# Late one-hots and the tail's table kept in program place on VectorE, and a portion's lists loaded expert by expert, in a convolution and mixture-of-experts kernel

## The chip, the cores and the metric

The kernel runs on one core of a Trainium2 chip. Its time is the device time in microseconds (us), from a set of runs; a profiled execution beside them shows where it goes. TensorE multiplies, VectorE (DVE) and ScalarE (ACT) move results out of PSUM, GpSimd (POOL) issues the indirect transfers, and SyncE (SP) issues most of the others. Each of these engines works off its own stream of instructions in order.

## The reference, cut to what matters

```python
w = softmax(weight, axis=-1)                    # [8 heads, 7 taps]
out[b, s, h*24:(h+1)*24] = sum_k w[h, k] * x_pad[b, s + k, h*24:(h+1)*24]   # causal, 7 taps
x = out.reshape(23040, 192)
g = argmax(x @ w_group)                         # 4 groups
e = argmax(x @ w_expert[g])                     # 4 experts in each group: 16 in all
y[token] = p_group * p_expert * (relu(x[token] @ w1[g, e]) @ w2[g, e])      # 192 -> 1024 -> 192
```

Each of the 23,040 tokens goes through one of 16 experts, which is known only once its logits are there.

## The kernel before

**Units.** The tokens are cut into 18 units, 0 to 17, of 4, 8 or 12 blocks of 120 tokens; units 8 to 17 have 12 blocks each. A unit (`unit`) is a Python generator. It convolves its blocks on TensorE, turns them, makes the logits, and routes on VectorE (L501 to L530); ACT then stores the convolved tokens to DRAM (`xcd`, L532). After some empty steps it works out each token's place in its expert's list (L545 to L557) and makes one-hots of that place, in halves of six blocks: `ohl` (L567), `ohr` (L571) and `ohv` (L575). TensorE multiplies these into a list of token numbers (L589), VectorE writes it out (L596, L598), and POOL scatters it into the table `idtab` in DRAM (L601). Each `yield` ends a step; steps are taken in between the matmuls of the expert stage, at a rate (`rate`, from `stages`) that has units done in time.

**Portions and slots.** The expert stage works on slots of 256 tokens of one expert. Slots come in portions: portion 0 (one slot for each expert) needs units 0 to 4, portion 1 (two for each) units 0 to 11, and portion 2 (two for each) all 18. `open_portion` loads the lists of token numbers of a portion from `idtab` into the tile `idp` (L1017: one transfer for each of the 16 experts on SP, from an address in a register). What is left over after portion 2 goes through a tail of 18 slots, 9 of them smaller, which a table (`table`) on VectorE and DRAM describes: for each tail slot its expert's weights and its place in `idtab`. `open_tail` makes the table and loads the tail's lists (L1035), a step at a time.

**A slot.** `open_slot(i + 2)` is called during slot i. It loads the expert's weights (L622 to L626), and POOL gathers the tokens from `xcd` (L673). `turn` transposes them (L686, L687) into `xa` and `xb` (L688 to L693). Four times `hidden` (L704, into `ph`, three PSUM banks) and `back` (L722, L726, into `po`, two banks) follow; ACT and VectorE split each result of `hidden` in `hh` and `hl` (L709, L710). VectorE splits the weights too (L639, L647, L654). At the end `ys` is made from `po` by ACT (L784) and VectorE (L785), and POOL scatters it to the output (L775). The next slot's first `back` needs `po` free, thus both `ys` of the slot before.

**Order.** The program gives an order, but the tool that builds the kernel sets each engine's final order itself: it simulates the kernel, and an instruction whose inputs are there in that simulation may go ahead of earlier ones that have to wait. `tc.keep_in_program_order(ins)` ties an instruction behind the instruction that was written just before it for the same engine. Transfers issued by SP and ACT count on a small set of semaphores that are handed out in turn; who takes one waits until the transfer that had it before has landed.

Of the kernel before, what the change touches and what calls it, by code (L numbers as in the profile page):

```python
# [20 lines left out]
P = 128  # L21
BT = 120
# [14 lines left out]
def conv_moe_kernel(  # L37
# [16 lines left out]
    PINA = True  # L54
    PINB = True
    PINW = True

    def pin(on, ins):

# [75 lines left out]
    UG = [0, 5, 6, 1, 5, 8, 0, 5, 6, 0, 5, 7, 0, 5, 6, 2, 5, 10]  # L135
    SK = [8, 8, 6, 11, 10, 9, 9]
    KPRE = [2, 150, 155, 160, 162, 20]
    CEU = 0
    CEH = (1, 3, 5, 7)
    PF = 1  # L140
# [235 lines left out]
    def unit(u, pre=None):  # L376
# [110 lines left out]
        def bc(a, n):  # L487
            return a.unsqueeze(len(a.shape)).broadcast_to([*a.shape, n])
# [40 lines left out]
        nc.vector.scalar_tensor_tensor(out=se, in0=se, scalar=1e-9, in1=sg, op0=ALU.add, op1=ALU.mult)  # L529
        nc.vector.reciprocal(out=xc[0:Q, 0:nb, 0], in_=se)  # L530
        xcw = xcd[t0:t0 + nb * BT, :].rearrange("(b p) d -> p b d", p=BT)
        SE.dma_start(out=xcw, in_=xc[0:BT, 0:nb, 0:XW])  # L532
        for _ in range(rest):
            yield
        while any(need <= u and pi not in idps for need, pi in needs.items()):
# [24 lines left out]
        halves = []  # L560
        for b0 in range(0, nb, HB2):
            n = min(HB2, nb - b0)
            ohl = pa.tile([P, HB2, P], F16, name="ohl", bufs=2)
            ohr = rt.tile([P, HB2, LH], F16, name="ohr", bufs=1)
            ohv5 = pa.tile([P, HB2, LH], F16, name="ohv", bufs=2)
            bs = slice(b0, b0 + n)
            nc.vector.tensor_tensor(  # L567
                out=ohl[0:Q, 0:n], in0=iop[0:Q].unsqueeze(1).broadcast_to([Q, n, P]), in1=bc(posb[0:Q, 0, bs], P),
                op=ALU.is_equal,
            )  # L570
            nc.vector.tensor_tensor(  # L571
                out=ohr[0:Q, 0:n], in0=ior[0:Q].unsqueeze(1).broadcast_to([Q, n, LH]), in1=bc(posb[0:Q, 1, bs], LH),
                op=ALU.is_equal,
            )
            OHE.tensor_tensor(  # L575
                out=ohv5[0:Q, 0:n], in0=ohr[0:Q, 0:n], in1=bc(vals[0:Q, bs], LH), op=ALU.mult)
            halves.append((b0, n, ohl, ohv5))
        rows = rt.tile([P, E + 1], F32, name="rows")
        rowi = rt.tile([P, 1], I32, name="rowi")
# [226 lines left out]
    flags = const.tile([P, 2], F32, name="flags")  # L806
    flagi = const.tile([P, 2], I32, name="flagi")

    def table(first=None, nbig=NBIG, nsmall=NSMALL):


# [5 lines left out]
        c = {n: const.tile([P, 1], F32, name=f"tc{g}_{n}") for n in ("j", "m1", "m2", "oa", "ob", "k", "ja", "jb")}  # L817
        ti = const.tile([P, E], I32, name=f"tb{g}_i")
        ji = const.tile([P, 1], I32, name=f"tc{g}_i")
        v = nc.vector  # L820

        def ts(out, in_, s1, op0, s2=None, op1=None):
            if op1 is None:
                v.tensor_scalar(out=out, in0=in_, scalar1=s1, scalar2=None, op0=op0)
            else:
                v.tensor_scalar(out=out, in0=in_, scalar1=s1, scalar2=s2, op0=op0, op1=op1)

        def tt(out, a, b, op):
            v.tensor_tensor(out=out, in0=a, in1=b, op=op)

        def stt(out, a, s, b, op0, op1):
            v.scalar_tensor_tensor(out=out, in0=a, scalar=s, in1=b, op0=op0, op1=op1)
# [9 lines left out]
        nc.gpsimd.iota(ti, pattern=[[1, E]], base=0, channel_multiplier=0)  # L842
        v.tensor_copy(out=t["eid"], in_=ti)
        v.memset(t["one"], 1.0)
        base = cons if first is None else first
        tt(t["rem"], ends[:, nends[0]], base, ALU.subtract)
        if first is None:


            cnt = rt.tile([P, UB * NG, EG], F32, name="dd").rearrange("p m e -> p (m e)")  # L850
            most = const.tile([P, 1], F32, name="most")
            for h in range(2):
                us = slice(h * NU // 2, (h + 1) * NU // 2)
                cn = cnt[:, 0:NU // 2 * E].rearrange("p (u e) -> p u e", e=E)
                tt(cn, ends[:, us.start + 1:us.stop + 1], ends[:, us], ALU.subtract)
                v.tensor_reduce(out=most if h == 0 else flags[:, 0:1], in_=cnt[:, 0:NU // 2 * E], axis=AX.X, op=ALU.max)
            tt(most, most, flags[:, 0:1], ALU.max)
            ts(flags[:, 0:1], most, float(SLOT), ALU.is_gt)
            ts(flags[:, 1:2], most, float(SLOT), ALU.is_le)
            ts(t["rem"], t["rem"], flags[:, 1:2], ALU.mult)  # L860
        slots(t["nf"], P - 1 if first is None else SLOT - 1)
        slots(t["ns"], SLOT - 1)
        tt(t["ns"], t["ns"], t["nf"], ALU.subtract)
        for n, pe, st in (("nf", "pa", "sa"), ("ns", "pb", "sb")):
            v.tensor_tensor_scan(t[pe], t["one"], t[n], 0.0, ALU.mult, ALU.add)
            tt(t[st], t[pe], t[n], ALU.subtract)
# [2 lines left out]
        ts(c["oa"], t["pa"][:, E - 1:E], -float(nbig), ALU.add, 0.0, ALU.max)  # L869
        ts(c["ob"], t["pb"][:, E - 1:E], -float(nsmall), ALU.add, 0.0, ALU.max)  # L870

        ts(c["m1"], c["j"], float(nbig), ALU.is_ge)
        ts(c["m2"], c["j"], float(ntail), ALU.is_ge)
        tt(c["k"], c["m1"], c["m2"], ALU.subtract)
        stt(c["ja"], c["m2"], -float(nsmall), c["j"], ALU.mult, ALU.add)
        stt(c["ja"], c["k"], -1024.0, c["ja"], ALU.mult, ALU.add)
        stt(c["k"], c["j"], -float(ntail), c["oa"], ALU.add, ALU.is_lt)
        stt(c["k"], c["k"], 1024.0, c["oa"], ALU.mult, ALU.add)
        tt(c["k"], c["k"], c["m2"], ALU.mult)
        stt(c["jb"], c["j"], -float(nbig), c["k"], ALU.add, ALU.subtract)  # L880
        for st, pe, j, m in (("sa", "pa", "ja", "ma"), ("sb", "pb", "jb", "mb")):
            ts(t["r"], t[pe], c[j], ALU.is_le)
            stt(t[m], t[st], c[j], t["r"], ALU.is_le, ALU.subtract)
# [4 lines left out]
        tt(t["q"], t["ma"], t["mb"], ALU.add)  # L888
        tt(t["q"], t["q"], t["eid"], ALU.mult)
        v.tensor_reduce(out=c["k"], in_=t["q"], axis=AX.X, op=ALU.add)  # L890
        ts(ent[:, 0:1], c["k"], float(D), ALU.mult)
        ts(ent[:, 1:2], c["k"], float(F), ALU.mult)

        ts(c["ja"], c["ja"], float(SLOT), ALU.mult, -float(DUMMY), ALU.add)
        stt(t["q"], t["sa"], -float(SLOT), base, ALU.mult, ALU.add)
        stt(t["q"], t["q"], c["ja"], t["ma"], ALU.add, ALU.mult)
        stt(t["r"], t["nf"], float(SLOT), base, ALU.mult, ALU.add)
        stt(t["r"], t["r"], -float(DUMMY), t["mb"], ALU.add, ALU.mult)
        tt(t["q"], t["q"], t["r"], ALU.add)
        v.tensor_reduce(out=c["k"], in_=t["q"], axis=AX.X, op=ALU.add)  # L900
        ts(ent[:, 2:3], c["k"], float(DUMMY), ALU.add)
# [24 lines left out]

    def stages(u):
        q = units[u][1] // QB
        return 1 + 8 + (2 * FRH if u >= FRU else 0) + sum(gaps(u)) + 3 * q + 1 + (LISTLAG if u >= NEED else 0)

    SKEW1 = 8
    LIVE1 = 3
# [54 lines left out]
    def open_tail():  # L987
# [4 lines left out]
        for j in range(NTAIL):  # L992
# [4 lines left out]
            tail_ids(row, idps["tail"][:, j], 2 if j < NBIG else 1)  # L997
            yield

    def open_portion(pi):  # L1000
        need, spe = portions[pi]
        rows = spe * 2
        idp = const.tile([P, E, rows, 1], I32, name=f"idp{pi}")
        if pi == 0:
            pin(PINI, IQ.dma_start(
                out=idp,
                in_=idtab[0:E * CAP].rearrange("(e r) c -> e r c", e=E)[:, 0:P * rows, :].rearrange(
                    "e (p r) c -> p e r c", r=rows),
            ))
        else:  # L1010
            ci = const.tile([1, E], I32, name=f"ci{pi}")
            nc.vector.tensor_copy(out=ci, in_=cons[0:1])
            _, base = nc.values_load_multi_w_load_instructions(
                ci, engines=[ET.SP], min_val=0, max_val=DUMMY - P * rows, skip_runtime_bounds_check_because=OOB_WHY,
            )
            for e in range(E):
                nc.sync.dma_start(  # L1017
                    out=idp[:, e],
                    in_=idtab[bass.ds(base[e], P * rows), :].rearrange("(p r) c -> p r c", r=rows),
                )  # L1020
        idps[pi] = idp
        consume(spe * SLOT)
        if pi + 1 == len(portions):
            late.append(open_tail())
# [38 lines left out]
    def open_slot(i):  # L1063
# [16 lines left out]
        if pi == "tail":  # L1080
            W = tail_weights(i)
            ids = idps["tail"][:, e]
            known = N
        else:
            W = pre.pop(e if pi == 0 else None, None) or weights(e * D, e * F, PENG(pi, e)) if s == 0 else opened[i - 1][0]
            ids = idps[pi][:, e, 2 * s:2 * s + 2]
            known = sum(n for _, n in units[:portions[pi][0]]) * BT
        for q in range(i + 1, i + 1 + TAHEAD):
# [21 lines left out]
    open_slot(1)  # L1110
    for e in range(2, 2 + PRE2):
        pre[e] = weights(e * D, e * F)
    for k in range(AHEAD):
        step()
    while opened[0][0]["todo"]:
        split_one(opened[0][0])
    unit_banks[:] = [(pm, "pm")]
    lead[:] = SKEW2, LIVE2
    turned[0] = turn(gathered[0])
    pinned[0] = False  # L1120
    pend = []
    tick = 0
# [10 lines left out]
    for i, (pi, e, s) in enumerate(plan):  # L1133
# [7 lines left out]
        for f2 in range(steps):  # L1141
# [27 lines left out]
            for q in range(f2, NF // 2, steps):  # L1169
                k = (q + 2) % 4  # L1170
                if q < 2:
                    split_one(W, k)
                elif i + 1 < len(plan):
                    split_one(opened[i + 1][0], k)
            if i + 1 < len(plan):
                if f2 == n - 1:
                    turned[i + 1] = turn(gathered[i + 1], tiles(i + 1))
# [93 lines left out]
```

## Time and profile before

| | |
|---|---|
| runs | 1166.22 us median of 3 (1163.81 to 1169.93) |
| the profiled execution | 1157.9 us; span from first to last instruction 1156.1 us |
| TensorE busy, mean granted clock | 96% of the span, 0.991 of full speed |
| VectorE, ScalarE, GpSimd busy | 70%, 60%, 43% |

The busy share of TensorE is high, but it is not the same everywhere: the rows below go by stretches. A row of the timeline gives the start in us from the start of the span, the duration, the engine, the line, and in brackets the idle time of the engine before it and what ended that.

### The profile page before, as it was taken

The page shows a single profiled execution, that of the slowest core. Times are in us where ns is not written, and L with a number is a line of the kernel's source. Part 1 is how long each engine was busy: PE and PEld are TensorE (multiplying, and loading weights), DVE is VectorE, ACT ScalarE, POOL GpSimd, SP SyncE. Part 2 cuts the span into 40 slices and gives each one's busy share as a digit, 9 for nine tenths or more (in the row PEclk, how much of TensorE's full clock was granted, in tenths as well). Part 3 has the DMA queues.
Part 4 walks back from the last instruction along what each step waited for, and adds up shares of the span by engine and source line. Part 5 has one row for each costly group of instructions (what it writes and reads, how often), then busy time and mean ns, then how long its engine had stood idle before and what let it go on. Part 6 is the DMA issues. An engine that isn't in the chain of part 4 may idle for free.

```text
span 1156.1 us, 23806 instructions
## 1 busy us (share of the span) xinstructions
PE 1105.5 (96%) x8468; PEld 1076.4 (93%) x8468; DVE 804.7 (70%) x1668; ACT 689.2 (60%) x1374; POOL 494.2 (43%) x443
## 2 busy tenths in 40 slices
PE   6887999989999999999999999999999999999996
PEld 5777999989999999999998999999999999989986
DVE  4777788877867666666678565666666666688874
ACT  5474666657565555655554555656555555677873
POOL 2121232435344443333344444444444445577773
PEclk9899999999999999999999999999999999999998
DMA  8869699889775554536364564544444546399970
GB/s 191 227 180 280 156 233 233 221 183 263 218 186 149 150 171 115 139 114 169 96 155 108 155 199 132 142 133 139 133 141 132 141 120 169 107 249 267 257 198 19
DMA packets 167212, 195.63 MB, mean 169 GB/s; under 512 B 22500, under 2 KB 144333, under 8 KB 167086
## 3 DMA queue, kind: packets, MB, share of 16 engines
q1 hardware_dynamic: 125006, 140.41, 46.0%
q0 software_dynamic: 18752, 35.85, 10.9%
q10 hardware_dynamic: 23328, 17.80, 6.4%
q8 instruction: 67, 1.10, 0.4%
q14 instruction: 59, 0.48, 0.1%
HBM read 158.79 MB, written 36.58 MB: 169 GB/s over the span
## 4 chain that ended last, share of the span: by engine, by line
PE 76%; DVE 8%; DMA 6%; issue 4%; ACT 3%; POOL 1%; SPq 0%; another core or an unknown queue 0%; POOLq 0%; ACTq 0%; DVEq 0%
PE ph L704 31%; PE po L722 20%; PE po L726 9%; PE pm L426 3%; PE pm L466 2%; DMA xg<-xcd,idpt 2%; PE pm L686 1%; PE pm L687 1%; DVE hl L710 1%; PE pm L445 1%; PE ph L739 1%; DVE cw L654 1%; PE pm L469 1%; DMA rawc<-in_moe_w 1%; DVE ohl L567 1%
## 5 line engine op out<-in xcount | busy, mean ns | idle before, releaser
L722 PE MATMUL po<-cw,hh 128*128 128x384 f32 x1424 | 442.3, 368 | 6.4 <-DVE ys L785 6.3
L704 PE MATMUL ph<-xa,ah 128*128 128x256 f32 x1424 | 390.1, 296 | 6.6 <-DVE xa L689 3.4
L775 POOL DMA_INDIRECT out<-ys,idp x160 | 169.2, 1057 | 449.2 <-DVE ys L785 336.6
L710 DVE SCALAR_TENSOR_TENSOR hl<-ph,hh 128x512 fp32r<-128x512 f32 x356 | 240.9, 685 | 169.9 <-ACT hh L709 155.8
L726 PE MATMUL po<-cw,hl 128*128 128x192 f32 x1424 | 356.8, 251 | 0.0
L709 ACT ACTIVATE hh<-ph 128x512 fp32r<-128x512 f32 x356 | 210.7, 594 | 212.6 <-PE ph L704 157.3
L704 PEld LDWEIGHTS ph<-xa,ah 128*128 128x128 f32 x1424 | 270.9, 190 | 9.6 <-DVE xa L689 3.6
L722 PEld LDWEIGHTS po<-cw,hh 128*128 128x128 f32 x1424 | 268.5, 189 | 10.3 <-DVE ys L785 8.2
L726 PEld LDWEIGHTS po<-cw,hl 128*128 128x128 f32 x1424 | 272.5, 191 | 1.6
L673 POOL DMA_INDIRECT xg<-xcd,idp x160 | 186.0, 1163 | 57.1 <-issue 28.7
L704 PE MATMUL ph<-xb,bh 128*128 128x256 f32 x712 | 202.0, 284 | 1.0 <-DVE xb L693 1.0
L704 PE MATMUL ph<-xb,bl 128*128 128x256 f32 x712 | 202.0, 284 | 0.0
L704 PE MATMUL ph<-xa,al 128*128 128x256 f32 x712 | 201.2, 283 | 0.0
L704 PEld LDWEIGHTS ph<-xa,al 128*128 128x128 f32 x712 | 136.5, 192 | 2.2
L704 PEld LDWEIGHTS ph<-xb,bh 128*128 128x128 f32 x712 | 136.2, 191 | 1.2 <-DVE xb L693 1.2
L704 PEld LDWEIGHTS ph<-xb,bl 128*128 128x128 f32 x712 | 136.9, 192 | 0.0
L654 DVE TENSOR_TENSOR cw<-rawc,cw 128x768 fp32r<-128x768 f32 x114 | 105.2, 953 | 14.9 <-ACT cw L653 11.9
L639 DVE TENSOR_TENSOR al<-raw,ah 128x1024 fp32r<-128x1024 f32 x57 | 70.8, 1242 | 35.8 <-ACT ah L638 19.6
L653 ACT ACTIVATE cw<-rawc 128x768 fp32r<-128x768 f32 x114 | 91.2, 839 | 3.0 <-DMA rawc<-in_moe_w 3.0
L785 DVE SCALAR_TENSOR_TENSOR ys<-po,xg,ys 128x192 f32<-128x192 f32 x187 | 76.0, 415 | 24.4 <-ACT ys L784 16.5
L692 ACT ACTIVATE xb<-pm 64x256 fp32r<-64x256 f32 x98 | 36.0, 368 | 94.8 <-DVE xa L689 89.1
L784 ACT ACTIVATE ys<-po,xg 128x192 f32<-128x192 f32 x187 | 76.1, 418 | 22.7 <-PE po L726 12.0
(223 smaller groups left out, 1552.5 us busy)
## 6 DMA issues: line engine op xcount, KB each, us to landing
rawc<-in_moe_w SPq DMA_DIRECT2D x114, 384.0 KB
raw<-in_moe_w SPq DMA_DIRECT2D x57, 512.0 KB
raw<-in_moe_w SPq DMA_DIRECT2D x114, 256.0 KB
xcd<-xc ACTq DMA_DIRECT2D x13, 1085.6 KB
xin<-in_x SPq DMA_DIRECT2D x7, 1134.0 KB
xc<-in_moe_w SPq DMA_DIRECT2D x18, 384.0 KB
xin<-in_x SPq DMA_DIRECT2D x6, 1039.5 KB
xin<-in_moe_w SPq DMA_DIRECT2D x9, 512.0 KB
```

What stands on the lines that cost most here:

```text
L639: eng.get(k, nc.vector).tensor_tensor(out=al, in0=ra, in1=ah.bitcast(F32), op=ALU.subtract)
L653: pin(PINW, nc.scalar.activation(out=cw[:, fs, 0, :], in_=rc[k - 2], func=AF.Copy))
L654: eng.get(k, nc.vector).tensor_tensor(out=cw[:, fs, 1, :], in0=rc[k - 2], in1=cw[:, fs, 0, :].bitcast(F32), op=ALU.subtract,)
L673: nc.gpsimd.indirect_dma_start(out=xs[:, t, :], out_offset=None, in_=xcd[0:known, :], in_offset=bass.IndirectOffsetOnAxis(ap=ids[:, t, 0:1 ...
L704: nc.tensor.matmul(out=hp[:, j], lhsT=wgt[:, fs], rhs=xx, start=i == 0, stop=i == len(ops) - 1)
L709: nc.scalar.activation(out=hh, in_=hp, func=AF.Relu)
L710: nc.vector.scalar_tensor_tensor(out=hl, in0=hp, scalar=0.0, in1=hh.bitcast(F32), op0=ALU.max, op1=ALU.subtract,)
L722: nc.tensor.matmul(out=oo[t][:, 0:2 * D], lhsT=hh[:, j, ts], rhs=cw[:, f].rearrange("p a d -> p (a d)"), start=f == 0, stop=False,)
L726: nc.tensor.matmul(out=oo[t][:, 0:D], lhsT=hl[:, j, ts], rhs=cw[:, f, 0, :], start=False, stop=f == NF - 1,)
L775: nc.gpsimd.indirect_dma_start(out=outviews[nscat[0] % len(outviews) if view is None else view], out_offset=bass.IndirectOffsetOnAxis(ap=i ...
L784: nc.scalar.activation(out=ys[:, t, :], in_=oo[t][:, D:2 * D], func=AF.Copy, scale=g)
L785: nc.vector.scalar_tensor_tensor(out=ys[:, t, :], in0=oo[t][:, 0:D], scalar=g, in1=ys[:, t, :], op0=ALU.mult, op1=ALU.add,)
```

## The change

One-hots of units 8 and later (`LP = 8`) are held: each is tied behind the VectorE instruction written before it. Their second half is written three steps after the first (`HGAP = 3`). The instructions of the tail's table are held too, the table has 11 more `yield`s, and its steps are also taken once within each slot of portion 2. The list loads of portions 1 and 2 are no longer written all at once in `open_portion`: `open_slot` writes those up to the expert after the one that it opens. `stages` counts the three steps. `LG`, `TB` and `SEV` are given values (0, 0 and 99) with which their code does nothing.

```diff
+    def hold(on, ins):
+        return tc.keep_in_program_order(ins) if on else ins
...
+    SEV = 99
+    TB = 0
+    HGAP = 3
+    LP = 8
+    LG = 0
+    IDN = 2
...
         for b0 in range(0, nb, HB2):
             n = min(HB2, nb - b0)
+            if u >= LP and b0:
+                for _ in range(HGAP):
+                    yield
...
-            nc.vector.tensor_tensor(
+            hold(u >= LP, nc.vector.tensor_tensor(
                 out=ohl[0:Q, 0:n], in0=iop[0:Q].unsqueeze(1).broadcast_to([Q, n, P]), in1=bc(posb[0:Q, 0, bs], P),
                 op=ALU.is_equal,
-            )
+            ))
...
+    class InOrder:
+        def __init__(self, on):
+            self.on = on
+        def __getattr__(self, name):
+            return lambda *a, **k: hold(self.on, getattr(nc.vector, name)(*a, **k))
...
-        v = nc.vector
+        v = InOrder(first is None)
...
         slots(t["nf"], P - 1 if first is None else SLOT - 1)
+        yield
         slots(t["ns"], SLOT - 1)
         tt(t["ns"], t["ns"], t["nf"], ALU.subtract)
+        yield
...
-        return 1 + 8 + (2 * FRH if u >= FRU else 0) + sum(gaps(u)) + 3 * q + 1 + (LISTLAG if u >= NEED else 0)
+        return 1 + 8 + (2 * FRH if u >= FRU else 0) + sum(gaps(u)) + 3 * q + 1 + (LISTLAG if u >= NEED else 0) + (HGAP + 2 * LG if u >= LP else 0)
...
+    idget = {}
+    def lists(pi, n):
+        while idget.get(pi) and E - len(idget[pi]) < n:
+            idget[pi].pop(0)()
...
-            for e in range(E):
-                nc.sync.dma_start(
-                    out=idp[:, e],
-                    in_=idtab[bass.ds(base[e], P * rows), :].rearrange("(p r) c -> p r c", r=rows),
-                )
+            idget[pi] = [lambda e=e: nc.sync.dma_start(
+                out=idp[:, e],
+                in_=idtab[bass.ds(base[e], P * rows), :].rearrange("(p r) c -> p r c", r=rows),
+            ) for e in range(E)]
...
             W = pre.pop(e if pi == 0 else None, None) or weights(e * D, e * F, PENG(pi, e)) if s == 0 else opened[i - 1][0]
+            lists(pi, e + IDN)
             ids = idps[pi][:, e, 2 * s:2 * s + 2]
...
+            if f2 == 2 and late and pi == len(portions) - 1 and len(idps) == len(portions):
+                next(late[0], None)
```

`ohr` and `ohv` are held in the same way as `ohl`, and nine further `yield`s stand between the later groups of the table's instructions.

## Rows read from the trace of the kernel before

**Rows 1.** Stretches: length, busy us of TensorE, weight loads, VectorE, ScalarE, GpSimd; granted clock.
```profile
260.00:628.00 368.00, 361.62 (x2841) 354.78 (x2840) 262.54 (x557) 212.07 (x422) 151.11 (x133) 1.00 0.58 157
628.00:1005.00 377.00, 377.00 (x2933) 376.99 (x2932) 239.59 (x386) 213.19 (x389) 167.45 (x158) 1.00 0.50 140
```
**Rows 2.** Waits of TensorE from 100 to 1005 us: total, times, longest.
```profile
PE po L722 <- DVE ys L785: 6.3, 6, 1.6
PE ph L704 <- DVE hl L710: 3.2, 1, 3.2
```
**Rows 3.** Timeline of TensorE around 250 us.
```profile
253.95 0.39 PE L704 MATMUL ph<-xa,ah 128*128 128x256 f32 x1 [3.20 <-DVE hl L710]
...
254.97 0.41 PE L704 MATMUL ph<-xa,ah 128*128 128x256 f32 x1
```
**Rows 4.** Timeline of ScalarE around 250 us.
```profile
252.15 0.32 ACTq L532 DMA_DIRECT2D xcd<-xc  x1
252.57 1.08 ACT L709 ACTIVATE hh<-ph 128x512 fp32r<-128x512 f32 x2 [7.50 <-DMA idp<-idtab]
```
**Rows 5.** The stretch after that wait; the last three numbers begin with the clock.
```profile
254.00:260.00 6.00, 6.00 (x32) 5.71 (x33) 5.33 (x7) 4.54 (x9) 0.00 (x0) 0.72 0.75 160
```
**Rows 6.** The list loads: duration min/median/max in ns, first and last start.
```profile
L1017 SPq DMA_DIRECT2D idp<-idtab x32: 238/333/1973, 247.4 to 628.7; - x32
```
**Rows 7.** Waits of SP's queue over the span: total, times, longest.
```profile
SPq L623 <- DVE al L639: 119.6, 27, 13.5
SPq L1017 <- DMA idtab<-lsi,rowi: 10.3, 2, 5.9
```
**Rows 8.** Timeline of TensorE: its six waits for `ys` from 260 to 628 us.
```profile
297.49 0.45 PE L722 MATMUL po<-cw,hh 128*128 128x384 f32 x1 [0.56 <-DVE ys L785]
...
323.40 0.44 PE L722 MATMUL po<-cw,hh 128*128 128x384 f32 x1 [1.58 <-DVE ys L785]
...
358.60 0.44 PE L722 MATMUL po<-cw,hh 128*128 128x384 f32 x1 [1.41 <-DVE ys L785]
...
496.62 0.45 PE L722 MATMUL po<-cw,hh 128*128 128x384 f32 x1 [0.37 <-DVE ys L785]
...
611.58 0.44 PE L722 MATMUL po<-cw,hh 128*128 128x384 f32 x1 [1.25 <-DVE ys L785]
...
623.44 0.45 PE L722 MATMUL po<-cw,hh 128*128 128x384 f32 x1 [1.15 <-DVE ys L785]
```
**Rows 9.** Timeline of VectorE, unit 13's one-hots at 355 us.
```profile
355.86 0.95 DVE L567 TENSOR_TENSOR ohl<-iop,posb 120x768 f16<-120x768 f32 x1
...
357.86 0.35 DVE L575 TENSOR_TENSOR ohv<-ohr,vals 120x192 f16<-120x192 f16 x1
358.13 0.41 DVE L785 SCALAR_TENSOR_TENSOR ys<-po,xg,ys 128x192 f32<-128x192 f32 x1
```
**Rows 10.** Timeline of VectorE, the table from 615 us: its first and last here.
```profile
615.56 0.23 DVE L824 TENSOR_SCALAR pos<-pos 128x16 f32<-128x16 f32 x1
...
620.99 0.15 DVE L824 TENSOR_SCALAR tb_e<-tc_k 128x1 f32<-128x1 f32 x1
```
**Rows 11.** Timeline of an undisturbed slot's end, VectorE and then TensorE.
```profile
699.47 0.96 DVE L785 SCALAR_TENSOR_TENSOR ys<-po,xg,ys 128x192 f32<-128x192 f32 x2
...
701.77 0.34 PE L722 MATMUL po<-cw,hh 128*128 128x384 f32 x1
```
**Rows 12.** Waits of TensorE from 0 to 100 us: total, times, longest.
```profile
PE ph L589 <- DVE ohv L575: 2.9, 1, 2.9
```
**Rows 13.** Timelines: unit 12's last `ohv`, its list's matmuls, slot 16's gather and turn.
```profile
293.42 0.34 DVE L575 TENSOR_TENSOR ohv<-ohr,vals 120x192 f16<-120x192 f16 x1
...
308.65 0.47 PE L589 MATMUL pm<-ohv,ohl 120*128 120x32 f16 x12
...
302.61 1.47 POOL L673 DMA_INDIRECT xg<-xcd,idp  x1 [0.30 <-ACT ta L447]
...
318.09 0.38 ACT L688 ACTIVATE xa<-pm 128x256 fp32r<-128x256 f32 x1
```

More of the change, by code (lines that the diff above doesn't have):

```diff
@@ L531, in unit @@
         xcw = xcd[t0:t0 + nb * BT, :].rearrange("(b p) d -> p b d", p=BT)
-        SE.dma_start(out=xcw, in_=xc[0:BT, 0:nb, 0:XW])
+        (nc.sync if u >= SEV else SE).dma_start(out=xcw, in_=xc[0:BT, 0:nb, 0:XW])
         for _ in range(rest):
@@ L566, in unit @@
             bs = slice(b0, b0 + n)
-            nc.vector.tensor_tensor(
+            hold(u >= LP, nc.vector.tensor_tensor(
                 out=ohl[0:Q, 0:n], in0=iop[0:Q].unsqueeze(1).broadcast_to([Q, n, P]), in1=bc(posb[0:Q, 0, bs], P),
                 op=ALU.is_equal,
-            )
-            nc.vector.tensor_tensor(
+            ))
+            if u >= LP:
+                for _ in range(LG):
+                    yield
+            hold(u >= LP, nc.vector.tensor_tensor(
                 out=ohr[0:Q, 0:n], in0=ior[0:Q].unsqueeze(1).broadcast_to([Q, n, LH]), in1=bc(posb[0:Q, 1, bs], LH),
                 op=ALU.is_equal,
-            )
-            OHE.tensor_tensor(
-                out=ohv5[0:Q, 0:n], in0=ohr[0:Q, 0:n], in1=bc(vals[0:Q, bs], LH), op=ALU.mult)
+            ))
+            hold(u >= LP, OHE.tensor_tensor(
+                out=ohv5[0:Q, 0:n], in0=ohr[0:Q, 0:n], in1=bc(vals[0:Q, bs], LH), op=ALU.mult))
             halves.append((b0, n, ohl, ohv5))
@@ L857, in table @@
             tt(most, most, flags[:, 0:1], ALU.max)
+            yield
             ts(flags[:, 0:1], most, float(SLOT), ALU.is_gt)
@@ L861, in table @@
         slots(t["nf"], P - 1 if first is None else SLOT - 1)
+        yield
         slots(t["ns"], SLOT - 1)
         tt(t["ns"], t["ns"], t["nf"], ALU.subtract)
+        yield
         for n, pe, st in (("nf", "pa", "sa"), ("ns", "pb", "sb")):
@@ L870, in table @@
         ts(c["ob"], t["pb"][:, E - 1:E], -float(nsmall), ALU.add, 0.0, ALU.max)
+        yield
         ts(c["m1"], c["j"], float(nbig), ALU.is_ge)
@@ L890, in table @@
         v.tensor_reduce(out=c["k"], in_=t["q"], axis=AX.X, op=ALU.add)
+        yield
         ts(ent[:, 0:1], c["k"], float(D), ALU.mult)
@@ L894, in table @@
         ts(c["ja"], c["ja"], float(SLOT), ALU.mult, -float(DUMMY), ALU.add)
+        yield
         stt(t["q"], t["sa"], -float(SLOT), base, ALU.mult, ALU.add)
         stt(t["q"], t["q"], c["ja"], t["ma"], ALU.add, ALU.mult)
+        yield
         stt(t["r"], t["nf"], float(SLOT), base, ALU.mult, ALU.add)
         stt(t["r"], t["r"], -float(DUMMY), t["mb"], ALU.add, ALU.mult)
+        yield
         tt(t["q"], t["q"], t["r"], ALU.add)
@@ L1112, in conv_moe_kernel @@
         pre[e] = weights(e * D, e * F)
-    for k in range(AHEAD):
+    for k in range(AHEAD - TB):
         step()
@@ L1116, in conv_moe_kernel @@
         split_one(opened[0][0])
+    if TB:
+        turned[0] = turn(gathered[0])
+    for k in range(TB):
+        step()
     unit_banks[:] = [(pm, "pm")]
     lead[:] = SKEW2, LIVE2
-    turned[0] = turn(gathered[0])
+    if not TB:
+        turned[0] = turn(gathered[0])
     pinned[0] = False
```

3 lines of the change are left out of this document (2 added, 1 removed).

## The prediction

> **What bounds the kernel now.** I read the stretches first, because a mean over the span hides that its parts have different limits. From 628 to 1005 us TensorE is busy for all of 377.00 us, with VectorE at 239.59, 64% of it; nothing that moves work about on VectorE can shorten that part. From 260 to 628 us, where the late units are convolved, routed and listed in between the slots, TensorE is busy for 361.62 of 368.00 us [rows 1]. TensorE is the bound in both, so only its idle time can be won. Then I read its waits from 100 to 1005 us: 6.3 us for `ys` (L785) in six waits, and 3.2 us for `hl` in one [rows 2]. (A wait of 4 us for the first slot's inputs, near 100 us, lies ahead of all late units and is left aside.) Last I went to each of these waits, and asked what VectorE or ScalarE had been doing.
>
> The single wait is at 250 us. TensorE stands for 3.20 us, and its next matmuls follow at a doubled duration (0.41 us) [rows 3]: the granted clock of the stretch from 254 to 260 us is 0.72 of full, so 2.4 GHz had fallen to 1.2 for a part of it [rows 5]. `hl` was late because ScalarE stood still for 7.50 us, which the profile puts down to the landing of a list load; the instruction that ScalarE issues right at the end of it is the store of unit 12's tokens, L532 [rows 4]. That store reads no list. What ties it to one is the semaphore: both take theirs from the same few, and 16 list loads in a row go through all of them. The first of these loads starts at 247.4 us [rows 6], after SP has waited for the scatter of a unit to land, which it does twice, up to 5.9 us [rows 7]. So the chain is: scatter, lists on SP, store on ScalarE, `hh`, `hl`, TensorE.
>
> The six waits for `ys` are 0.56, 1.58, 1.41, 0.37, 1.25 and 1.15 us [rows 8], 6.32 in all. In the one at 358 us VectorE makes unit 13's one-hots from 355.86, and the second `ys` has to wait until 358.13 [rows 9]. In the last one the table ran from 615.56 to 621.14 us, with only two `hl` and a list in it [rows 10]; `xa`, `xb` and `ys` come behind. The waits at 297, 496 and 611 us have one-hots ahead of them in the same way. The one of 1.58 us at 323 us has not: there VectorE is in unit 13's routing, and ScalarE in the store that follows.
>
> **The change part by part.** It adds and removes no instruction of an engine: the same 32 list loads, one-hots and table. Only places move. `LG`, `TB` and `SEV` cost nothing, because no code runs for them.
>
> Lists, one by one. At 240 to 260 us SP has two loads (experts 0 and 1) instead of 16. The store's semaphore then last served something that was issued before the lists, and that has landed, unless just enough other loads come in between. Lists from expert 2 on are written after unit 12's scatter, whose table they read, and so can't drift forward to 247 us. What is won is the wait, 3.20 us, and the slow clock behind it: 0.72 over 6 us means 56% of it, 3.4 us, at half speed, so 1.7 us of work lost. Together 4.9 us. The bounds: 0, if the store is caught by one of the two loads; 4.9, if it is free. I take 4.9, since there are 14 lists fewer ahead of the store. In portion 2 the 16 loads cost TensorE nothing now (it is full from 628 us on, with loads until 628.7 [rows 1, 6]), so nothing is won there.
>
> What the later loading costs. Each of the lists from expert 2 on is written two slots, about 20 us, ahead of the gather that reads it; the longest wait of SP's queue is 13.5 us [rows 7], so it is hidden. The first one of a portion is written in the same call as its gather. For slot 16 the gather's second part ends at 304.08 and the turn starts at 318.09 [rows 13]: 14.0 us of cover. I put this at nothing. If the first list came behind the longest SP wait and took 2 us to land, 1.5 us would be lost.
>
> The Trainium skill, "DMA: Bandwidth & Descriptors", section Rules for kernel authors, speaks against this part: it says to issue a transfer early, compute, and wait late. By that rule the 16 early loads are right, and the sum without this part's term would be 4.9 us smaller; here the row of ScalarE's 7.50 us shows an early transfer holding up another one, which the rule does not speak of.
>
> The second halves. A half costs VectorE 0.95 + 0.35 + 0.35 = 1.65 us (the second 0.35 by `ohv`'s row, which has the same size as `ohr`) [rows 9]. The first half's `ohl` is tied only behind the instruction that makes its own input, so it drifts forward as before; it is the second half that leaves the block. The four waits with one-hots ahead, 0.56 + 1.41 + 0.37 + 1.25 = 3.59 us, are each shorter than 1.65 us, so each of them goes to zero where the rest keeps its place. What is late next: the second half itself, three steps later. In an undisturbed slot the second `ys` ends at 700.43, and TensorE needs the bank from 701.77 [rows 11]: 1.34 us to spare. A half that falls right before `ys` costs 0.3 us; for ten units, and a quarter of the slot in which it could hurt, that is an estimate of 0.8 us. Net 2.8 us; bounds 0 (each unit just gets stuck elsewhere) and 3.6. The list's matmuls wait for the second `ohv`, but they are at 308.65 where `ohv` ended at 293.76 [rows 13], and the eight empty steps in between stay: 15 us of cover against the 7 or so that three steps take.
>
> The table. Its instructions stay in portion 2, after 628 us, in pieces of up to nine, 0.15 to 0.23 us each [rows 10], so 1.5 us at most. They are written behind `hl` of the first and third quarter of a slot, not before `ys`, and VectorE is idle for a third of that stretch [rows 1]. So the wait of 1.15 us goes and nothing comes in its place; bounds 0.5 (a piece now and then meets a `ys`) and 1.15. The table is done at about slot 58 and the tail's lists by slot 67, well ahead of slot 80, which needs them.
>
> The sum: 4.9 + 2.8 + 1.15 = 8.9 us less. Against the profiled execution (1157.9 us, of which 1.8 lie around the span) this makes 1149.0. The median of the runs shown is 8.3 us above that execution; taken from it, 1166.2 - 8.9 = 1157.3 us.
>
> **The rivals.** First, the store stays caught: the two early loads, or a load of weights that is stuck behind them on SP, hold its semaphore. For it speaks that SP still waits for the scatter; against it that 14 of 16 loads are gone. Then 2.8 + 1.15 = 4.0 us are won: 1162.2.
>
> Second, the change doesn't do what it says. The final order is simulated afresh; one-hots and routing of other units come before a `ys`, as the routing did at 323 us for 1.58 us [rows 8], and a store gets caught elsewhere for part of the time. Gains of 0 to 2 us: about 1165. The Trainium skill, "Perfetto Trace Analysis", section Identifying the Most-Contended Engine, says to optimize the engine with the highest occupancy first; the change leaves TensorE's work alone, and by that rule the time would stay. The idle time in the rows is what the rule leaves out.
>
> Third, slower: TensorE comes to wait for the held halves. In its first 100 us it waited up to 2.9 us for `ohv` before a list (L589) [rows 12]. If the final order keeps those matmuls where they are and the halves slip, ten units cost up to 29 us; it decides against the change from an average of about 1.5 us for each of the ten, which eats the 8.9 and 5.8 more. Against it stand the 15 us of cover. The time would be about 1175. A store caught in each of three more units, at 4.9 us each, would come to much the same (1172), as lists now wait for the scatters of units 12 to 17 one by one.
>
> **How the numbers follow.** Forecast 0.53, store still caught 0.20, little change 0.15, slower 0.12. A measurement of this kernel can tell about 0.5%, 5.8 us, from no change: faster means below 1160.4, slower above 1172.0. Of the forecast 0.50 lies below 1160.4, of the first rival 0.04, so 0.54 faster; slower is 0.09 of the third rival's 0.12 and a little of the second, 0.11; the rest, 0.35, is the same. The likeliest case's own range: all bounds at their best, 4.9 + 3.6 + 1.15 with the wait at 323 us gone too, make 11.2 us, 1155; with the run-to-run spread 1152. At their worst, 1161. The range goes on to the second rival and the spread above it, 1168.
>
> **What would show it.** Right: in 240 to 260 us no idle time of ScalarE that ends with a list load, a granted clock of 1.00, and list loads spread to 600 us; no table on VectorE before 628 us; half of a late unit's one-hots some 5 us behind the other; fewer and shorter waits for `ys`. Wrong: L532 behind a list again, TensorE waiting for `ohv` at L589 or for `xa` behind a gather, or new waits for `ys` after 628 us.

## The result, and the profile after

The changed kernel takes 1147.87 us (median of four executions, 1146.75 to 1152.56) beside 1165.01 us for the kernel before: ratio 0.9875, 95% interval 0.9829 to 0.9921. Forecast were 1157.3 us and a range that began at 1152. The direction was right. The forecast gain was 8.9 us, and the measured one is 14.6 us by the ratio and 17.1 by the medians. The profiled execution took 1148.97 us, against 1157.9 for that of before.

One stretch of before that [rows 1] does not have, then the stretches of after, with the same columns:

```profile
240.00:260.00 20.00, 16.80 (x114) 16.05 (x113) 12.87 (x27) 9.46 (x20) 4.71 (x5) 0.91 0.75 173
```
```profile
240.00:260.00 20.00, 20.00 (x157) 19.32 (x157) 16.24 (x36) 12.71 (x28) 7.72 (x8) 1.00 0.98 249
260.00:628.00 368.00, 366.79 (x2889) 360.60 (x2887) 259.59 (x509) 215.16 (x423) 155.72 (x139) 1.00 0.57 157
628.00:1005.00 377.00, 376.80 (x2919) 375.98 (x2918) 247.77 (x444) 215.36 (x393) 167.50 (x155) 1.00 0.51 141
```

From 260 to 628 us TensorE's busy time rose from 361.62 to 366.79 of 368. From 240 to 260 us it stands nowhere and the granted clock is 1.00, where it had been busy for 16.80 us of 20 at a clock of 0.91. After 628 us nothing could be won and nothing was; VectorE's 58 instructions more there are mostly the table.

TensorE's waits from 100 to 1005 us, which answer to [rows 2]:

```profile
PE ph L720 <- DVE xa L705: 3.4, 1, 3.4
PE ph L720 <- issue: 1.0, 3, 0.5
PE ph L720 <- DVE xb L709: 0.8, 1, 0.8
PE pm L436 <- ACT xc L445: 0.4, 1, 0.4
PE po L738 <- DVE ys L801: 0.2, 1, 0.2
```

The wait for `hl` is gone, and of 6.3 us for `ys` 0.2 are left. (The 3.4 us for `xa` are the first slot's inputs near 100 us, which the prediction had left aside.)

ScalarE around unit 12's store, now L542, answers to [rows 4]; then SP in the same stretch, to [rows 6] (ACTq and SPq mark what an engine's queue issues):

```profile
245.65 0.32 ACTq L542 DMA_DIRECT2D xcd<-xc  x1
246.52 0.38 ACT L708 ACTIVATE xb<-pm 64x256 fp32r<-64x256 f32 x1 [1.99 <-DVE xa L705]
```
```profile
249.21 2.37 SPq L1058 DMA_DIRECT2D idp<-idtab  x2
251.69 1.72 SPq L642 DMA_DIRECT2D rawc<-in_moe_w  x2
```

No idle time of ScalarE ends with a list load any more. But the reader should see the order too: the store is issued 3.6 us ahead of the first list, where before it came 4.8 us behind it. Unit 13's one-hots, which answer to [rows 9], are the two halves that the prediction spoke of, 3.5 us apart, the second still right ahead of `ys`:

```profile
347.26 0.95 DVE L580 TENSOR_TENSOR ohl<-iop,posb 120x768 f16<-120x768 f32 x1
...
350.75 0.96 DVE L580 TENSOR_TENSOR ohl<-iop,posb 120x768 f16<-120x768 f32 x1
...
352.01 0.36 DVE L591 TENSOR_TENSOR ohv<-ohr,vals 120x192 f16<-120x192 f16 x1
352.29 0.74 DVE L801 SCALAR_TENSOR_TENSOR ys<-po,xg,ys 128x192 f32<-128x192 f32 x2
```

The table runs on VectorE from 649.27 us; before, most of it ran from 606 to 622 us, the first part ahead of the wait at 611 us, which the prediction gave to one-hots alone.

The two traces differ by 8.9 us, the medians by 17. The traces also differ in their start. ScalarE's copies `xa` of slots 0 and 80 in after:

```profile
98.92 0.42 ACT L704 ACTIVATE xa<-pm 128x256 fp32r<-128x256 f32 x1
...
983.06 0.38 ACT L704 ACTIVATE xa<-pm 128x256 fp32r<-128x256 f32 x1
```

That is 884.1 us from slot 0 to slot 80, against 98.06 to 990.77, 892.7 us, before. Slot 0 comes at 94.0 to 98.5 us in the five traces of the kernel before below and at 98.9 to 101.9 us in three of after, and the work behind slot 80, which the change leaves alone, took 163.2 to 167.2 us in the traces of before alone. From slot 0 to slot 80 the five traces of before take 891.1 to 898.2 us, mean 893.7, and the three of after 879.5, 884.1 and 884.5, mean 882.7: 11.0 us less, with nothing of the start's and the tail's scatter in it.

### The profile page after: what moved, and what is told of

It is laid out like the page before. It is cut to its first block, busy times and chain, and to the rows that moved or that the text cites. A ratio compares the mean times of both kernels' runs of the same rounds, so it can differ in the third digit from the quotient of the medians.

```text
span 1147.2 us, 23807 instructions
## 1 busy us (share of the span) xinstructions
PE 1107.6 (97%) x8468; PEld 1078.0 (94%) x8468; DVE 805.2 (70%) x1668; ACT 690.5 (60%) x1374; POOL 498.7 (43%) x443
## 4 chain that ended last, share of the span: by engine, by line
PE 85%; DVE 4%; DMA 4%; issue 3%; ACT 3%; SPq 0%; POOL 0%; POOLq 0%; ACTq 0%; DVEq 0%
PE ph L720 35%; PE po L738 22%; PE po L742 10%; PE pm L436 4%; PE pm L476 3%; PE pm L702 2%; PE pm L703 2%; DMA xin<-in_x 1%; PE pm L455 1%; PE ph L755 1%; DMA xg<-xcd,idpt 1%; PE pm L479 1%; DMA xcd<-xc 1%; PE ph L436 1%; DVE cw L670 1%
## 5 line engine op out<-in xcount | busy, mean ns | idle before, releaser
L670 DVE TENSOR_TENSOR cw<-rawc,cw 128x768 fp32r<-128x768 f32 x114 | 105.3, 954 | 14.8 <-ACT cw L669 10.7
```

Of the source, the lines that this page charges most:

```text
L670: eng.get(k, nc.vector).tensor_tensor(out=cw[:, fs, 1, :], in0=rc[k - 2], in1=cw[:, fs, 0, :].bitcast(F32), op=ALU.subtract,)
```

## The experiments

In the expectations A says that the profiled execution of before was a mild one, and that the caught store costs more in most; B that the same waits were there and the difference lies in the start or the clock; C that the three empty steps between a unit's halves do the one-hots' part; D that holding the instructions does it. All ratios are to the kernel before, run on the same chip; they are those on record, and differ a little from the quotients of the medians.

**The kernel before again.** No edit.

> The kernel before, unchanged, to see what its runs differ in. Theory A (the profiled execution was a mild one, and the caught store of unit 12 costs more in most runs, since how long SP waits for the scatter differs from run to run): this profile shows the wait of TensorE near 250 us longer than 3.2 us, and the time is 1160 to 1170 us. Theory B (all runs lose the same in the waits, and what differs lies in the first 100 us or in the clock): the wait near 250 us is 3.2 us again, and the rest of the difference to 1157.9 us lies elsewhere. Ratio to the kernel before 1.000.

0.9992 (0.9959 to 1.0025), 1160.95 us; the kernel before beside it 1161.7 over 31 executions, 4.5 us less than the 1166.2 from which the prediction took its sum (sets of runs differ by chip, as the last section shows). The waits of this execution:

```profile
PE po L722 <- DVE ys L785: 7.4, 6, 1.6
PE ph L704 <- DVE hl L710: 4.3, 1, 4.3
```

Together 11.7 us where [rows 2] has 9.5. A is right for this trace; the three later traces of the same kernel have less than [rows 2], so it does not hold in general.

**One part at a time.** The lists' part alone (`open_portion` and `lists`), the one-hots' part alone (`hold` on three instructions, three empty steps, the added count of `stages`), the table's part alone (`InOrder` and the `yield`s).

> The kernel before with only the lists loaded expert by expert. Theory A: this part is most of the gain, 9 to 12 us (ratio 0.990 to 0.992). Theory B: it gives 4.9 us (ratio 0.996), as summed from the profiled execution. The rival that the store stays caught: ratio 1.000.

0.9947 (0.9916 to 0.9978): 6.2 us by the ratio, 4.8 by the medians. TensorE still waits 7.6 us for `ys`, and 2.2 us for `hl` at 289 us. There ScalarE waits 4.5 us for raw weights (`rawc`), which SP issued at 275.91, 20 us behind the two lists, and which landed only at 288.80: no list holds them.

> The kernel before with only the one-hots of units 8 and later held and their second halves three steps later; lists and table as before. Theories A and B both: 2.8 to 3.6 us (ratio 0.997), the four waits for ys with one-hots ahead of them gone, the caught store still there. Rival (the order is only simulated afresh): ratio 1.000, waits for ys elsewhere.

0.9943 (0.9913 to 0.9974): 6.6 us by the ratio (8.4 by the medians), more than twice the term of 2.8; the interval begins at 3.0. `ys` is waited for 2.7 us in all. And the store is not caught, though 16 lists are loaded at once: it is issued at 246.18, the lists from 249.03.

> The kernel before with only the tail's table in program place, in smaller portions. Theories A and B both: 1.2 us (ratio 0.999), the wait for ys at 622 us gone, the others there. Rival (the table pushes more than its one wait shows): 3 us or more (ratio 0.997).

1.0003 (0.9975 to 1.003). The table runs from 662.66 us and its own wait is gone, and so are those at 297 and 496 us, but the ones at 328 and 618 us have grown to 2.3 and 1.5 us (5.3 in all), and `hl` costs 6.5 us in two waits, 2.3 of them new, behind `rawc` that landed late.

**Within the one-hots' part.** Steps without holding, then holding without steps (`HGAP = 0`):

```
def hold(on, ins):
    return ins
```

> The kernel before with only the three steps between the halves of a late unit's one-hots (and their count in the rate), nothing held. Theory C (the three steps do it: they part the halves, and they shift the units' steps against the opening of portion 1, so that unit 12's store comes ahead of the lists): ratio 0.994, as with the one-hots' part whole, and no wait of TensorE at 250 us. Theory D (holding does it; without it the second half drifts forward to the first): ratio 0.998 to 1.000.

> The kernel before with the one-hots of units 8 and later held, both halves in one step as before. Theory C: ratio 1.000, the block ahead of ys as long as before, the store at 250 us caught. Theory D: ratio 0.994 to 0.996.

Steps alone 0.9968 (0.9945 to 0.9991), 3.7 us; holding alone 0.9997 (0.9971 to 1.0023). First the steps' waits, then those of holding:

```profile
PE ph L720 <- DVE hl L726: 2.8, 1, 2.8
PE po L738 <- DVE ys L801: 2.6, 3, 1.4
```
```profile
PE po L738 <- DVE ys L801: 6.5, 6, 1.6
PE ph L720 <- DVE hl L726: 4.5, 2, 4.3
```

Holding alone shows no gain, so D is wrong. C is right in what the trace shows: with nothing held the steps take `ys` to 2.6 us, where the first two traces of before have 6.3 and 7.4, and the store, issued at 246.22, comes ahead of the lists. In time the steps alone reach only about half of C's 0.994; whether holding adds anything to them (0.9943 beside 0.9968, on two chips) lies within the intervals. The steps also count in `stages`, from which the rate of all steps is set, and no run parted the two. The 2.8 us for `hl` at 266 us are new: ScalarE waits 6.2 us there for `rawc`, which SP issues behind the 16 lists. This is a second cost of loading them at once, and the prediction has no word of it.

**The whole again, and without the lists' part.** The second is after with `open_portion` as before.

> The changed kernel, unchanged, beside the other runs of this call. If its parts add up (lists 6.1 us, one-hots 6.6, table 0), the ratio to the kernel before is 0.989; if the parts help each other, as fewer waits at once would, it is 0.987 or below. If lists and one-hots free the same store twice over, so that the second to come wins nothing there, it is 0.993. Its profile: no wait of TensorE over 0.5 us between 105 and 628 us; the time to the first slot's start differs by several us from the other profile of it.

> The changed kernel with all lists of a portion loaded at once again. If the lists' part is worth nothing once the one-hots' part has moved the store: the same as the changed kernel of this call within 0.2%. If it is worth its own 6 us: 0.5% above it, with waits of TensorE from 260 to 628 us behind weights that came late, since SP is held for 12 us by 16 list loads.

0.9884 (0.9851 to 0.9917), and without the lists 0.994 (0.9909 to 0.9971). The parts add up: 0.9947 x 0.9943 x 1.0003 is 0.9893. The lists are worth 0.56% on top of the others, as much as alone (0.53%; the two intervals of this pair overlap a little), although the steps have already moved the store ahead of them. What is left to win is the weights: without the lists' part ScalarE waits 3.9 us for `rawc` and 2.9 for `raw` from 240 to 300 us, and TensorE 1.7 us for `hl` in two waits; in the whole ScalarE waits for no `rawc` there, and TensorE has no wait over 0.15 us from 108.1 to 1005 us. (Ahead of that the first slot's inputs cost it 3.0 and 1.0 us, where none over 0.5 was expected from 105 us on.)

**The store by itself.** The kernel before with one line changed, the store of unit 12 on another queue, all 16 lists at once:

```
-        SE.dma_start(out=xcw, in_=xc[0:BT, 0:nb, 0:XW])
+        (nc.gpsimd if u == 12 else SE).dma_start(out=xcw, in_=xc[0:BT, 0:nb, 0:XW])
```

> The kernel before with one line changed: the store of unit 12's tokens is issued by GpSimd instead of ScalarE. All 16 lists still load at once, TensorE's, SP's and the other engines' orders stay, except for a few local swaps. If ScalarE's stand of 7.5 to 8.6 us behind a list load is what costs, it is gone from ScalarE, TensorE's wait at 250 us (3.2 to 4.3 us) and the half clock behind it go with it, and about 5 us are won: 1156, ratio 0.995. If the 16 loads cost in a second way too, by holding SP for 12 us so that weights land late, ScalarE then waits 3 to 6 us for raw weights near 265 us, TensorE idles for about 3 us there, and only 2 us are won: 1159, ratio 0.998. Rival: the stand only moves to GpSimd and the gathers of the next slots come late: 1161 or more, with waits of TensorE behind a gather.

0.9991 (0.997 to 1.0011): nothing. TensorE, ScalarE and SP in this kernel, from their timelines:

```profile
264.50 0.58 PE L704 MATMUL ph<-xa,ah 128*128 128x256 f32 x1 [3.68 <-DVE hl L710]
```
```profile
253.84 0.83 ACT L653 ACTIVATE cw<-rawc 128x768 fp32r<-128x768 f32 x1
262.01 0.84 ACT L653 ACTIVATE cw<-rawc 128x768 fp32r<-128x768 f32 x1 [7.33 <-DMA rawc<-in_moe_w]
```
```profile
245.97 12.04 SPq L1017 DMA_DIRECT2D idp<-idtab  x16
258.11 0.94 SPq L626 DMA_DIRECT2D rawc<-in_moe_w  x2
```

ScalarE no longer stands at 250 us, and TensorE then stands 3.68 us at 261 us instead: the 16 loads hold SP for 12.04 us, the weights are issued behind them, and `cw`, `hh` and `hl` are late by that way. The two causes lie one behind the other, and the first had covered most of the second.

> The kernel before with one line changed: the store of unit 12's tokens is issued by SP instead of ScalarE. In SP's order it comes with four weight loads among the 16 lists, so the weights no longer stand behind all 16. If stand and late weights are the two costs of loading the lists at once, both are smaller here: no idle time of ScalarE that ends with a list load and waits for raw weights under 3 us; about 5 us won, 1156, ratio 0.995, and not above the run with the store on GpSimd. Rival: the store waits for VectorE on SP, all behind it is late, and nothing is won: 1161.

The same line with `nc.sync`: 1.0028 (1.0007 to 1.0048), a miss. ScalarE, then SP:

```profile
265.54 0.84 ACT L653 ACTIVATE cw<-rawc 128x768 fp32r<-128x768 f32 x1 [11.11 <-DMA rawc<-in_moe_w]
```
```profile
245.64 7.26 SPq L1017 DMA_DIRECT2D idp<-idtab  x12
253.00 0.42 SPq L532 DMA_DIRECT2D xcd<-xc  x1
253.53 1.33 SPq L626 DMA_DIRECT2D rawc<-in_moe_w  x1
```

SP has 12 lists and the store ahead of the first weights, so these go out 4.6 us earlier than with the store on GpSimd. Yet they land later: by the semaphore that ScalarE waits for, this `rawc` (384 KB), issued at 253.53 right behind the store of 1,086 KB, landed at 265.52, 12.0 us after its issue, against 3.9 us in the kernel with the store on GpSimd. TensorE waits 7.5 us for `hl`. Late weights decide in both kernels, once by a late issue and once by a slow landing; that the store's bytes slow it is likely and not shown.

**Fewer lists at once.** The lists' part with `IDN = 8` instead of 2, then with the store on GpSimd too.

> The kernel before with 8 of portion 1's lists at once and the others expert by expert. The 8 loads hold SP for about half of 12 us, so weights are issued some 6 us earlier than behind 16. If the stand of ScalarE comes from loads that go through all of a few semaphores, and 8 loads are too few for that or their landing is earlier, ScalarE's idle time behind a list load is under 3 us, TensorE has no wait over 1 us from 240 to 270 us, and most of the lists' part is won: 0.9955. Rival: 8 still catch the store; idle time of ScalarE of 4 us or more with DMA idp as its releaser, a wait of TensorE near 250 us, and a ratio within 0.2% of 1.

> As e13, and the store of unit 12 issued by GpSimd. If stand and late weights lie one behind the other, taking the store off ScalarE wins nothing when 16 loads hold SP (e9) but lets the whole of the lists' part show here: 0.995, no wait of TensorE over 1 us from 240 to 270 us. If 8 loads never caught the store, this is e13 again, within 0.2%. Rival: late weights were not the second cost; then TensorE's wait near 261 us is as long as in e9 (3.7 us) and the ratio is that of e9, 0.999.

0.9969 (0.9946 to 0.9993) and 0.9945 (0.992 to 0.9969). The store behind eight lists, from ScalarE's timeline of the first:

```profile
252.44 0.32 ACTq L532 DMA_DIRECT2D xcd<-xc  x1
252.87 1.09 ACT L709 ACTIVATE hh<-ph 128x512 fp32r<-128x512 f32 x2 [4.25 <-issue]
```

ScalarE stands 4.25 us ahead of the store instead of 7.5; the profile names no releaser, but by the trace's records ScalarE waits there for the semaphore that the first of the eight lists took. TensorE has no wait at 250 us and one of 1.8 us at 288. With the store on GpSimd it waits 0.2 us for `hl`, and the ratio is that of the lists' part (0.9945, beside 0.9947 with two lists), though `ys` still costs 8.1 us. With 16 loads, freeing the store won nothing; with eight the middle values differ by 0.24%, but the intervals overlap. 0.9945 and 0.9947 lie clear of 1 and 0.9991 does not; the three are from three chips.

**The whole without one part.**

> The changed kernel without the one-hots' part: lists expert by expert and the table held, no three added steps. If the parts add up, this is the lists' part alone (0.9947) plus the table (0): 0.9947, about 1155, and the missing one-hots cost some 7 us against the whole change (0.9884). Rival: lists and steps free the same store, so that one of them is spare: then this is close to the whole change, 0.990 or below, 1149.

> The changed kernel with the table left to float as in the kernel before. By the prediction's term it costs 1.15 us: 0.9894, 1148.5, with the table on VectorE before 628 us and a wait of TensorE for ys of about 1 us at 620 us. By the run of the table alone (1.0003) it costs nothing: 0.9884, 1147.3. Rival: in the whole, where no other wait is left to grow in its place, the floating table costs more than its own wait: 0.992 or above, 1151.5.

Without the one-hots 0.9938 (0.9916 to 0.9959): as the lists and the table added up (0.9947), and not the rival's 0.990 or below. Its `ys` waits are only 2.6 us, with no steps in it, and `hl` costs 2.5 us behind a `rawc` that landed 13.7 us after its issue. Without the table 0.9911 (0.9877 to 0.9944). There the table floats to 596 to 607 us, and its wait is in the trace as expected:

```profile
598.72 0.45 PE L738 MATMUL po<-cw,hh 128*128 128x384 f32 x1 [1.42 <-DVE ys L801]
599.76 0.44 PE L738 MATMUL po<-cw,hh 128*128 128x384 f32 x1 [0.22 <-DVE ys L801]
```

On this chip the kernel before took 1153.53 us, and after was not run there, so the two ratios can't be set against 0.9884 from another. Set against each other (1147.80 and 1144.86 us), the one-hots' part is worth 2.9 us more than the table's on top of the lists, with intervals that overlap.

**Both once more side by side, and before twice more.**

> The changed kernel again, beside the kernel before on the same chip. If the gain belongs to the order of the program: a ratio of 0.984 to 0.993 whatever the chip, no wait of TensorE over 0.5 us from 108 to 1005 us, and 857 to 861 us from slot 2 to slot 80. Rival: on a chip where the kernel before takes 1153.5 us, its waits are shorter and the ratio is 0.993 or above.

> The kernel before again, for its trace. Its waits by theory: 3.2 to 4.3 us for hl at 250 us behind ScalarE's stand, 6 to 7.5 us for ys from 260 to 628 us, 871 to 876 us from slot 2 to slot 80, ratio 1 within 0.3%. Rival: on a chip where it takes 1153.5 us one of these is gone, and slot 2 to slot 80 takes under 868 us.

After 0.9855 (0.9827 to 0.9882), 1150.45 us; before 1.0006 (0.9984 to 1.0028), 1166.75 us. One `ys` wait of 1.36 us is left in after, and one of 0.7 us with no cause that the profile shows, where under 0.5 was expected, and slot 2 to slot 80 takes 862.7 us, a little above the 857 to 861 named. The trace of before shows no more waits than the first (`hl` 2.6, `ys` 6.7 us), but it is of an execution of 1157.2 us, the fastest of its twelve.

> The kernel before once more, for its trace. If longer executions differ in the waits that the change takes away, a span above 1160 us goes with waits of TensorE of 4 us or more at 250 us and over 7 us for ys from 260 to 628 us. Rival: they differ in the first 119 us or after 1005 us, with slot 2 to slot 80 within 871 to 876 us as in the traces so far.

> As e17: the same kernel and the same two readings, on the same chip.

0.999 (0.9969 to 1.0011) and 0.9982 (0.9944 to 1.0021), medians 1154.3 and 1155.1 us; the two profiled executions took 1151.54 and 1155.97 us, none over 1160, so the question was not answered. They have only four `ys` waits, 5.2 and 4.6 us, the one near 322 us is missing, and `hl` costs 3.5 and 3.0 us. So the five traces of before have 9.5, 11.7, 9.3, 8.7 and 7.6 us of these waits, in the order in which they were taken: the one that the prediction was made from was not a mild one.

**All traces side by side.** From slot 2 to slot 80 (ScalarE's copies `xa` again) the traces sort by the three steps. With the steps: 861.0, 857.8 and 862.7 us for after, 858.5 without the table, 861.7 without the lists, 862.1 for the one-hots' part alone, 867.8 for the steps with nothing held. Without the steps: 870.2 to 875.9 for before, 871.4 for the lists alone, 871.5 and 872.1 for eight lists at once, 870.5 and 873.6 with the store moved, 873.4 with holding alone, 877.6 with the table alone; lists and table together, 865.9, lie between. So the lists' part alone, 6.2 us by its ratio, does not show in its trace: one wait goes, and others are as long or longer. Each kernel but two has a single trace here, and those of before differ by 5.7 us, so why time and trace disagree stays open.

## Why the prediction was wrong in size

**Where the time is.** Right: TensorE bounds both stretches, and the idle time won is that of [rows 2]. Added up with the half-clocked stretch, 6.3 + 3.2 + 1.7, it is 11.2 us, which the prediction named as the best case; 0.2 us of `ys` is left, so 11.0 us were won there. The same two traces differ by 10.7 us from slot 2 to slot 80 (871.7 and 861.0).

**Lists, 4.9 us.** Measured 6.2 by the ratio and 4.8 by the medians alone, and on top of the others 5.4 by the medians (1152.7 and 1147.3) or 6.5 by the ratios (0.56%), so in time the term was of the right size; in the traces it is not to be seen. The chain behind it was half of the story. "The chain is: scatter, lists on SP, store on ScalarE, `hh`, `hl`, TensorE" holds for the kernel before, but with the store taken out of it nothing was won; a second chain, lists on SP, weights, `cw`, `hh`, `hl`, ended 3.68 us late by itself. The prediction looked at what the loads did to a semaphore, not at what stood behind them on SP. It would have failed for a change that moved the store alone. What the chain says of the semaphore the trace of before bears out. Ahead of the store, ScalarE has a wait of its own at L532:

```profile
L532 ACTq EVENT_SEMAPHORE  x1: 17/17/17, 252.1 to 252.1; - x1
```

In the trace's records this wait is for the semaphore that the seventh list load, issued at 250.52, counts on. It ended when that load landed, at 252.07, and the store, issued at 252.15, then counts on the same one. The 16 list loads go through eight such semaphores.

The Trainium skill, "DMA: Bandwidth & Descriptors", section Rules for kernel authors, says that small transfers should be coalesced, since under 64 KB one pays mostly overhead. The row of 12.04 us for 16 lists of 2 KB, 0.75 us each, agrees: the two weight loads behind them, of 384 KB each, took 0.94 us together. By its rule one load of all lists would cost less than any order of 16. No run here tried that, and the lists lie at addresses of their own. The same section's rule to issue early and wait late, which the prediction weighed against this part, is the one that the measurements contradict here: later was better by 0.5% in time (0.9947, 0.9916 to 0.9978).

**Second halves, net 2.8 us.** This is the first step that failed. The part measured 6.6 us by the ratio (3.0 to 10.1 by its interval, beside the term's own bounds of 0 and 3.6), 3.7 of it with steps alone; from slot 2 to slot 80 the traces put nearly all that is won with the steps. (On top of the lists, with the table taken as nothing, it is 2.9 us on one chip, with a wide interval.) Four waits were counted, those with one-hots right ahead, the one at 323 us was left standing, and 0.8 us was charged for halves that meet the next `ys`. In the runs the sum of `ys` waits is 4.1 to 8.1 us in every kernel with neither steps nor the table's part, and 0 to 2.7 us in every kernel with the steps, where new waits for `ys` stay under 0.8 us. (Lists and table without the steps come to 2.6 as well, the table alone to 5.3.) The second thing was not seen at all: three steps more in a unit shift what the program writes near it, so that unit 12's store is issued ahead of the lists. The prediction took the steps for a distance between two halves and nothing else.

**The table, 1.15 us.** Its wait is real (1.15 in [rows 8], 1.42 where the rest of the change stands), and it goes. In time it shows nothing: alone, other waits came in its place; in the whole, 0.1% is less than these measurements tell. (Nine pieces of up to 0.23 us make 2.1 us, not the 1.5 of the prediction.)

**The sum and its base.** 8.9 us against the profiled execution made 1149.0, and the profiled execution of after took 1148.97. That is luck: 10.7 us were won from slot 2 to slot 80 and 1.3 behind it, and in after slot 2 came 3.0 us later. The second step that failed is the last one, taking 8.9 us from the median of the runs shown. Even the best case of the waits, 11.2 us, gave 1155 by that step, 7 us above the result; the kernels' medians lie 13.7 to 17.1 us apart in three comparisons. The executions of before lay above their trace in three sets of runs (1161 to 1167 against 1157 to 1159; in a fourth, 1154 to 1156 against 1151.5 and 1156.0), those of after at it or below (1147.3, 1147.9 and 1150.5 against 1148.3, 1149.0 and 1152.6). So by the traces a part of the gain lies in executions of before that no trace shows. Extra waits of the same kind are seen in one trace (2.2 us more than in [rows 2]), and less of them in three. What is on record of the others is their granted clock: on the chip where the profiled execution of before was the fastest of twelve, it has 1157.20 us at 0.991, and the slowest 1173.67 at 0.982; among 31 on another chip the fastest has 1156.35 at 0.991, the slowest 1171.32 at 0.980. Reckoned as in the prediction, where a stretch at half speed loses half of its length, 0.009 of 1160 us gives an estimate of 10 us of the 16 between the first two. Between the kernels the mean clock differs less (0.9864 and 0.9892 on the first of these chips, an estimate of 3 us; 0.9886 and 0.9892 on a third, under 1), so where the rest sits stays open.

**The rivals.** The store was not caught in any kernel with two lists at once; in each it was issued ahead of the first list, by 1.1 to 4.3 us, so whether two loads could hold it was not put to the test. TensorE waited for no held one-hot. Gathers behind the first list of a portion were not late either; SP waits for scatters five times instead of twice, 30.7 us instead of 10.3, with no wait of TensorE behind them.

## What to carry to other kernels

When a wait has one cause in the trace, ask what else would have been late a few microseconds later, on each queue that the cause occupies: here a burst of 16 small loads held a store on one engine and the weights on its own queue, and moving the store alone won nothing. A few empty steps between two blocks of work move everything that is written around them, so compare the order of all engines, not the distance alone. And size a gain from several traces of the kernel before, in a stretch that leaves out start and tail; the profiled execution may be the shortest of a dozen, and a gain in time that no trace shows is a gain whose cause is not known yet.

## What the runs showed of the hardware

Sixteen list loads of 2 KB held SP for 10.7 to 12.6 us, eight for 6.8 and 8.3, two for 0.9 to 2.6. A store on ScalarE that reads none of them stood 6.9 to 8.6 us behind sixteen and 4.3 behind eight; the trace of before has ScalarE waiting there for the very semaphore of a list load (its end at 252.07 us, the store at 252.15), and no run took the semaphore itself away. A weight load of 384 KB landed 3.9 us after its issue in one kernel and 12.0 us in another, right behind a store of 1,086 KB on the same queue. The same kernel before had medians of 1153.5, 1156.1, 1161.1, 1161.7 and 1166.1 us on five chips, a spread of 1.1%, as much as the change is worth, so that only executions side by side on one chip could be compared.
